# Attention and gated MLP on one core: filling work put ahead of transposes, weight splits one step later, last copies of the first MLP in other buffers

## The chip, the cores and the metric

One core of a Trainium2 chip runs the whole program. The metric is the device time of one execution in microseconds (us); what is compared is the median of several runs. Engines are named as in the profile: PE (TensorE, PEld its weight loads), DVE (VectorE), ACT (ScalarE), POOL (GpSimd), SP (SyncE, which issues the DMAs of this kernel in its own order, SPq in the rows).

## What is computed

```python
def _attn_ref(q, k, v):                      # 8 batches, 8 heads, 576 rows, head size 64
    k_p = k.reshape(B, H, S // 8, 8, D).mean(axis=3)
    v_p = v.reshape(B, H, S // 8, 8, D).mean(axis=3)
    scores = np.matmul(q, k_p.transpose(0, 1, 3, 2)) / np.sqrt(D)
    attn = np.exp(scores - np.max(scores, axis=-1, keepdims=True))
    attn = attn / (np.sum(attn, axis=-1, keepdims=True) + 1e-09)
    return np.matmul(attn, v_p)

def _moe_ref(x, w_gate, w_val, w_out):       # x 4608 x 512, 1536 hidden
    gate = 1.0 / (1.0 + np.exp(-(x @ w_gate)))
    return gate * (x @ w_val) @ w_out

def _moe2_ref(x, w_in, w_out):               # 2048 hidden
    h = x @ w_in
    return np.where(h > 0.0, h, np.exp(np.minimum(h, 0.0)) - 1.0) @ w_out

x = attention(q, k, v) as 4608 rows of 512
out = _moe2_ref(_moe_ref(x, ...), ...)
```

Weights come as 64-bit floats and are narrowed on the chip.

## The kernel before, in words

The 4608 rows are cut into 12 blocks of 384, a block into three tiles of 128. A matmul of full precision is made of three passes of a faster format, with an upper part (a rounded copy, ACT, line 95) and a lower part (source minus upper part, line 96, mostly on POOL). So each weight, each activation `g` and each `x` is "split" before PE can use it.

**Attention of the first two blocks** (lines 617 to 695) comes first and has PE nearly to itself. Per tile `t`: `emit_s` (scores on PE, maximum and subtraction on DVE), `emit_exp` (ACT), `emit_norm` (sum and reciprocal on DVE, product on POOL), `emit_t` (five transposes on PE, split of the transposed probabilities `pt` by ACT and DVE). `between(t)` holds work that fills: pooling K and V by sums of 8 rows (`pool_k`, `pool_v`: five DVE reductions each), `emit_k` (transposes of pooled K, copied to `kbd`), `emit_q`, `place_v` (pooled V spread into masked tiles `vbd` on POOL), and weight conversions. `emit_pv` makes the output `x` of a block.

**Weights of the first MLP** are 36 jobs, three for each of 12 chunks of hidden columns (gate, value, out). A job is loaded as 512 KB of raw words (`fetch`), opened (`open`: ACT takes magnitudes into a tile `nt`), narrowed by four DVE instructions (`narrow_1`, lines 108 and 112; `narrow_2`, lines 118 and 122) and split into `wg` or `wo`. One call of `convert` moves the pipeline by a step: it loads ahead, opens job i+1, does the second half of job i-1 and the first half of job i, and splits job i-1:

```python
            fetch_to(i + 1 + ahead)
            open_to(i + 1 + peek)
            turns = [narrow_2(j.raw, j.t) for j in upto("two", i)] + [narrow_1(j.t) for j in upto("one", i + 1)]
            for _ in range(2):
                for t in turns:
                    next(t, None)
            split_to(i)
```

`nt` has three buffers. Raw words go alternately to the two `raw` buffers and to free `wo` slots, the last five jobs to `raw` alone. The order of the instructions on each engine is that in which the code calls them; engines wait for one another by semaphores.

**First chunk loop** (lines 809 to 830): for each chunk `c`, both gates of block 0 (24 matmuls of 384 columns), three calls of `convert`, the output product of block 0's previous chunk (12), both gates of block 1's previous chunk (24, kept in DRAM as `gd`). That makes 60 matmuls a chunk. Scores of block 2 and block 1's output products (`second_y`, which takes `g` back from DRAM) follow in lines 857 to 877; then come blocks 2 to 11.

**Start of the second MLP** (from line 1021): a step ("slot") is one of seven products of six matmuls (`product`, line 960), then some matmuls from the list `fill`, then what ACT and DVE do behind it (`behind`). In the first seven slots `fill` holds the last 12 output products of the first MLP, from slot 7 on output products of the second (`oacc`, line 1006), which take the accumulators that `flush_y` (lines 537 to 544) empties in slot 6. `flush_y` copies four accumulators to `yo`, a row buffer (4 of them, 3 of which `t_p1`, `t_u2` and `t_u3` hold by then), and stores each to DRAM.

## Time and profile before

| what | us |
|---|---|
| median of 3 runs | 1930.62 (1929.45 to 1930.74) |
| profiled execution | 1932.92, of which span 1931.2 |
| start of the first gate in the profile | 87.14 |
| start of the second MLP in the profile | 1153.48 |

The span runs from the first to the last instruction; what lies around it is 1.7 us. The profiled execution is 2.3 us above the median.

### The profile page before, as it was taken

The page shows a single profiled execution, that of the slowest core. Times are in us where ns is not written, and L with a number is a line of the kernel's source. Part 1 is how long each engine was busy: PE and PEld are TensorE (multiplying, and loading weights), DVE is VectorE, ACT ScalarE, POOL GpSimd, SP SyncE. Part 2 cuts the span into 40 slices and gives each one's busy share as a digit, 9 for nine tenths or more (in the row PEclk, how much of TensorE's full clock was granted, in tenths as well). Part 3 has the DMA queues.
Part 4 walks back from the last instruction along what each step waited for, and adds up shares of the span by engine and source line. Part 5 has one row for each costly group of instructions (what it writes and reads, how often), then busy time and mean ns, then how long its engine had stood idle before and what let it go on. Part 6 is the DMA issues. An engine that isn't in the chain of part 4 may idle for free.

```text
span 1931.2 us, 25883 instructions
## 1 busy us (share of the span) xinstructions
PE 1840.8 (95%) x9996; PEld 1736.9 (90%) x9996; DVE 881.2 (46%) x1455; ACT 793.3 (41%) x1565; POOL 509.0 (26%) x523
## 2 busy tenths in 40 slices
PE   4689789999999999999999997999999999999999
PEld 3589779999999999999999996999989999999997
DVE  6698335454444543455543132443444344443432
ACT  3344224334434343444433233444454444544443
POOL 1454222222113122123222111222222222222222
PEclk7799889999999999999999998999999999999999
DMA  7144223232312322242320424334353343343430
GB/s 185 59 141 150 79 82 90 79 113 71 96 61 80 120 72 77 96 123 91 100 88 28 158 77 188 118 138 160 120 190 123 123 184 115 144 150 144 157 115 33
DMA packets 119227, 218.21 MB, mean 113 GB/s; under 512 B 44352, under 2 KB 76096, under 8 KB 119104
## 3 DMA queue, kind: packets, MB, share of 16 engines
q1 hardware_dynamic: 119104, 216.56, 33.0%
q8 instruction: 78, 1.28, 0.3%
q14 instruction: 45, 0.37, 0.1%
HBM read 172.23 MB, written 44.30 MB: 112 GB/s over the span
## 4 chain that ended last, share of the span: by engine, by line
PE 87%; DVE 4%; DMA 3%; ACT 2%; issue 2%; SPq 1%; POOL 1%; ACTq 0%; DVEq 0%; POOLq 0%
PE gv L507 28%; PE oacc L1006 20%; PE bank L960 18%; PE acc L526 14%; PE atv L487 2%; PE xv L487 2%; PE ats L416 1%; SPq L319 1%; PE att L460 1%; DVE ks L356 1%; PE atq L406 1%; DMA rkv<-in_k_dram 1%; DMA yd<-yo 1%; DMA rkv<-in_v_dram 1%; DVE vs L375 1%
## 5 line engine op out<-in xcount | busy, mean ns | idle before, releaser
L507 PE MATMUL gv<-x,wg 128*128 128x384 f32 x3456 | 643.2, 340 | 14.8 <-ACT sg L515 9.2
L507 PEld LDWEIGHTS gv<-x,wg 128*128 128x128 f32 x3456 | 604.6, 190 | 19.2 <-ACT sg L515 11.1
L1006 PE MATMUL oacc<-w2o,gc 128*128 128x512 f32 x1728 | 453.8, 394 | 1.9 <-DVE yo L541 1.6
L1006 PEld LDWEIGHTS oacc<-w2o,gc 128*128 128x128 f32 x1728 | 320.3, 188 | 50.7 <-DVE yo L541 2.0
L960 PE MATMUL bank<-form,wr 128*128 128x384 f32 x1728 | 355.0, 340 | 9.4 <-ACT p L982 7.9
L960 PEld LDWEIGHTS bank<-form,wr 128*128 128x128 f32 x1728 | 316.1, 189 | 33.1 <-ACT p L982 8.4
L526 PE MATMUL acc<-g,wo 128*128 128x384 f32 x1728 | 331.3, 340 | 8.4 <-ACT g L95 5.7
L96 POOL TENSOR_TENSOR g<-sg,g 128x384 fp32r<-128x384 f32 x132 | 144.3, 1093 | 663.3 <-ACT g L95 663.3
L526 PEld LDWEIGHTS acc<-g,wo 128*128 128x128 f32 x1728 | 304.9, 190 | 12.5 <-ACT g L95 6.4
L519 DVE TENSOR_TENSOR sg<-sg,gv 128x384 f32<-128x384 f32 x132 | 72.5, 549 | 276.1 <-PE gv L507 274.4
L96 POOL TENSOR_TENSOR gc<-ea,gc 128x384 fp32r<-128x384 f32 x96 | 98.0, 1021 | 300.0 <-ACT gc L95 295.9
L96 POOL TENSOR_TENSOR gc<-eb,gc 128x384 fp32r<-128x384 f32 x96 | 98.1, 1022 | 271.4 <-ACT gc L95 250.9
L515 ACT ACTIVATE sg<-gv 128x384 f32<-128x384 f32 x144 | 70.6, 490 | 216.0 <-PE gv L507 213.4
L95 ACT ACTIVATE g<-sg 128x384 fp32r<-128x384 f32 x132 | 69.2, 524 | 158.5 <-DVE sg L519 158.5
L96 DVE TENSOR_TENSOR pt<-att,pt 128x512 fp32r<-128x512 f32 x72 | 34.5, 486 | 119.5 <-ACT pt L95 119.5
L969 ACT ACTIVATE ea<-bank 128x384 f32<-128x384 f32 x48 | 23.6, 492 | 158.4 <-PE bank L960 158.4
L973 DVE SCALAR_TENSOR_TENSOR ea<-ea,bank 128x384 f32<-128x384 f32 x48 | 26.6, 555 | 117.7 <-ACT ea L970 117.7
L969 ACT ACTIVATE eb<-c 128x384 f32<-128x384 f32 x48 | 25.2, 525 | 131.6 <-DVE c L990 131.6
L95 ACT ACTIVATE gc<-eb 128x384 fp32r<-128x384 f32 x96 | 50.4, 525 | 56.6 <-DVE eb L973 33.3
L95 ACT ACTIVATE gc<-ea 128x384 fp32r<-128x384 f32 x96 | 50.5, 526 | 55.4 <-DVE ea L973 55.4
L984 DVE TENSOR_TENSOR u<-p,bank 128x384 f32<-128x384 f32 x48 | 26.6, 554 | 98.9 <-PE bank L960 96.7
L960 PE MATMUL bank<-formx,wr 128*128 128x384 f32 x288 | 58.4, 337 | 0.0
(107 smaller groups left out, 1868.6 us busy)
## 6 DMA issues: line engine op xcount, KB each, us to landing
wr<-wd SPq DMA_DIRECT2D x96, 896.0 KB, 6.2
rw<-in_moe_w_out_dram SPq DMA_DIRECT2D x23, 512.0 KB, 3.8
yd<-yo SPq DMA_DIRECT2D x48, 192.0 KB, 2.1
r<-yd SPq DMA_DIRECT2D x24, 384.0 KB, 8.0
out_dram<-po SPq DMA_DIRECT2D x36, 256.0 KB, 2.0
rw<-in_moe_w_in_dram SPq DMA_DIRECT2D x16, 512.0 KB, 4.5
wd<-rw SPq DMA_DIRECT2D x16, 512.0 KB, 3.3
wod<-rw SPq DMA_DIRECT2D x16, 512.0 KB, 2.7
```

Source lines behind the costliest of these rows:

```text
L95: nc.scalar.activation(out=dst_hi, in_=src, func=AF.Copy)
L96: eng.tensor_tensor(out=dst_lo, in0=src, in1=f32(dst_hi), op=ALU.subtract)
L487: nc.tensor.matmul(d[j][:, o:o + w], lhsT=vb[:m, a_w].rearrange("p e d -> p (e d)"), rhs=p[a_p][:m, j + e, o:o + w], start=(e == 0 and a_w ...
L507: nc.tensor.matmul(d, lhsT=w[:, i, a_w, j], rhs=x[:, a_x, j], start=(j == 0 and a_w == 0 and a_x == 0), stop=(j == KD - 1 and a_w == 1),)
L515: nc.scalar.activation(out=sg, in_=gps, func=AF.Sigmoid)
L519: nc.vector.tensor_tensor(out=sg, in0=sg, in1=vps, op=ALU.mult)
L526: return lambda: nc.tensor.matmul(acc[m], lhsT=wo[c][:, a_w, m * P:(m + 1) * P], rhs=g[:, a_g], start=(c == 0 and a_w == 0 and a_g == 0), ...
L960: nc.tensor.matmul(bank[b ^ flip], lhsT=wp[q][a_w][:, w, j * P:(j + 1) * P], rhs=form_tile(s, a)[j][:, a_x], start=opens and n == 0, stop= ...
L969: nc.scalar.activation(out=e, in_=src, func=AF.Relu, scale=-1.0)
L973: nc.vector.scalar_tensor_tensor(out=e, in0=e, scalar=-1.0, in1=src, op0=ALU.add, op1=ALU.max)
L984: nc.vector.tensor_tensor(out=u2, in0=t_p1, in1=src, op=ALU.add)
L1006: return lambda: nc.tensor.matmul(acc[t + i], lhsT=g[c][:, a_g, i * P:(i + 1) * P], rhs=wo2[2 * q + e][:, a_w], start=opens and p == 0, st ...
```

## The change

Six edits.

1. The first three weight jobs are loaded earlier: job 0 ahead of all keys, job 1 ahead of the queries, job 2 ahead of the second block's keys. Seven instead of five conversions are done before the first chunk loop.
2. In the attention of the first two blocks, `emit_exp` and `between(t)` stand ahead of `emit_t(t - 1)`; what `between` holds is dealt out anew.
3. `convert` begins with the split of job i-2 instead of ending with that of job i-1. Every fourth `nt` is a row buffer (`ntr`).
4. Even jobs at the end also load to free `wo` slots.
5. In `second_y`, the split of `g` stands ahead of the tile's `emit_exp`.
6. `flush_y` of the last block is due in slot 3; its last three copies go to `nt` buffers (`yn`); all 12 fill matmuls are issued in slot 3, none in the other slots before 7.

```diff
+    turn = [0]
+    def first_t():
+        turn[0] += 1
+        return row_tile("ntr", DM).bitcast(I32) if turn[0] % 4 == 0 else plain_t()
@@ fetch_to
-            if i % 2 or i > 3 * C1 - 6:
+            if i % 2:
                 job.raw = raw_tile("rw")
@@ convert
+            split_to(i - 1)
             fetch_to(i + 1 + ahead)
...
-            split_to(i)
@@ flush_y
-            t = row_tile("yo", NB)
+            if n == NBLK - 1 and m:
+                t = act.tile([P, DM], F32, name="yn", tag="nt", bufs=3)[:, :NB]
+            else:
+                t = row_tile("yo", NB)
@@ loads
+        fetch_to(1)
         load_all("k", 0, k0, l0[:, 0])
+        fetch_to(2)
         for i in range(TPB):
             load_q(i, q0[:, i])
+        fetch_to(3)
         load_all("k", 1, k1, l1[:, 0])
-        fetch_to(1)
...
+        convert(1, 0, 0)
         for c in range(NCH):
             pool_k(0, c)
         emit_k(0)
+        open_to(2)
         for i in range(TPB):
             emit_q(i, qt[0][:, i])
+        convert(1, 0, 0)
@@ between
             if t == 0:
+                convert(1, 1, 0)
+            elif t == 1:
                 for c in range(NCH):
                     pool_k(1, c)
-            elif t == 1:
+            elif t == 2:
                 emit_k(1)
-                for c in range(3):
-                    pool_v(0, c)
-            elif t == 2:
-                convert(1, 2)
-                for c in range(3, NCH):
+                for c in range(NCH):
                     pool_v(0, c)
...
-                convert(1, 2)
-                for j in range(HP):
-                    place_v(0, j)
+                place_v(0, 2)
+                place_v(0, 3)
+                convert(1, 1)
@@ tiles
             scores = emit_s(t, ph[t])
+            emit_exp(scores)
+            between(t)
             if t > 0:
                 emit_t(t - 1, True)
-            emit_exp(scores)
-            between(t)
             emit_norm(t, scores)
-            if t == TPB:
+            if t == TPB - 1:
+                place_v(0, 0)
+                place_v(0, 1)
+            elif t == TPB:
                 emit_pv(0)
@@ second_y
                     load_g(done + 2)
+                if then:
+                    then()
+                    then = None
                 if pend:
                     last_y()
...
-            emit_exp(scores)
-            second_y(1)
+            second_y(1, lambda: emit_exp(scores))
@@ second MLP
-        due = {6: [lambda: flush_y(pn, pacc)]}
+        due = {3: [lambda: flush_y(pn, pacc)]}
...
-                    filler(-(-len(fill) // (7 - k)))
+                    filler(len(fill) if slot == 3 else -(-len(fill) // (7 - k)) if slot > 6 else 0)
```

On DVE, at tile 1 of the attention, before: maximum and subtraction of the scores, then at once the split of tile 0's transposed probabilities (`pt`).

```order
L424 TENSOR_REDUCE mx<-ats 128x8
L427 TENSOR_TENSOR p_211<-ats,mx 128x576
L96 TENSOR_TENSOR pt<-att_251,pt 128x4x128
L96 TENSOR_TENSOR pt<-att_252,pt 64x128
L370 COPY kbd_126<-atk 64x4x72
L375 TENSOR_REDUCE vs<-v_133 128x64 x3
L438 TENSOR_REDUCE sm<-p_211 128x8
```

The same place in the changed kernel:

```order
L431 TENSOR_REDUCE mx<-ats 128x8
L434 TENSOR_TENSOR p_225<-ats,mx 128x576
L363 TENSOR_REDUCE ks<-k_131 128x64 x4
L363 TENSOR_REDUCE ks<-l_136 64x64
L96 TENSOR_TENSOR pt<-att_275,pt 128x4x128
L96 TENSOR_TENSOR pt<-att_276,pt 64x128
L445 TENSOR_REDUCE sm<-p_225 128x8
```

The five reductions of block 1's keys now stand between the subtraction and the split of `pt`; the copy `kbd` and the sums of V have gone to tile 2.

On ACT, in the first chunk loop, from the split of block 0's second `g` on, before:

```order
L95 ACTIVATE g<-sg 128x384
L190 ACTIVATE nt<-rw 128x512
L95 ACTIVATE wg_767<-nt 128x512
L515 ACTIVATE sg<-gv 128x384 x2
L190 ACTIVATE nt<-rwo 128x512
L95 ACTIVATE wg_767<-nt 128x512
```

And in the changed kernel:

```order
L95 ACTIVATE g<-sg 128x384
L95 ACTIVATE wg_763<-nt 128x512
L197 ACTIVATE nt<-rw 128x512
L522 ACTIVATE sg<-gv 128x384 x2
L95 ACTIVATE wo_845<-ntr 128x512
L197 ACTIVATE nt<-rwo 128x512
```

The upper part (`wg`, `wo`) stood behind the opening of the next job and right ahead of the sigmoids (`sg`); now it is that of a job one step older, ahead of the opening.

On PE, slots 3 to 5 of the second MLP, before (line 960 is `product`, line 526 the first MLP's output products):

```order
L960 MATMUL bank_10033<-form_9860,wr_9549 128x384 x2
L960 MATMUL bank_10033<-form_9860,wr_9550 128x384
L526 MATMUL acc<-g,wo_1696 128x384 x2
L960 MATMUL bank_10032<-form_9910,wr_9549 128x384 x2
L960 MATMUL bank_10032<-form_9910,wr_9550 128x384
L960 MATMUL bank_10032<-form_9910,wr_9549 128x384 x2
L960 MATMUL bank_10032<-form_9910,wr_9550 128x384
L526 MATMUL acc<-g,wo_1696 128x384 x2
```

And in the changed kernel:

```order
L978 MATMUL bank_10033<-form_9860,wr_9549 128x384 x2
L978 MATMUL bank_10033<-form_9860,wr_9550 128x384
L533 MATMUL acc<-g,wo_1624 128x384 x12
L978 MATMUL bank_10032<-form_9910,wr_9549 128x384 x2
L978 MATMUL bank_10032<-form_9910,wr_9550 128x384
L978 MATMUL bank_10032<-form_9910,wr_9549 128x384 x2
L978 MATMUL bank_10032<-form_9910,wr_9550 128x384
```

All twelve matmuls of the first MLP's last output now stand behind slot 3's product, and none behind slot 4's.

## Rows read from the trace of the kernel before

**Rows 1.** The page: busy time of each engine over the span.

```profile
PE 1840.8 (95%) x9996; PEld 1736.9 (90%) x9996; DVE 881.2 (46%) x1455; ACT 793.3 (41%) x1565; POOL 509.0 (26%) x523
```

**Rows 2.** Windows: length, busy us (instructions) of each engine, PEclk, DMA share, GB/s.

```profile
core 0: us, PE busy (x) PEld busy (x) DVE busy (x) ACT busy (x) POOL busy (x), PEclk, DMA share, GB/s
0.00:87.14 87.14, 40.37 (x193) 33.53 (x193) 53.57 (x84) 29.43 (x71) 27.70 (x47) 0.72 0.47 127
87.14:117.73 30.59, 25.07 (x121) 23.82 (x121) 26.85 (x38) 13.61 (x25) 13.27 (x9) 0.89 0.37 120
117.73:180.96 63.23, 63.07 (x361) 62.75 (x361) 58.20 (x84) 28.12 (x55) 35.57 (x24) 1.00 0.49 158
...
189.35:213.64 24.29, 16.60 (x74) 15.95 (x74) 10.64 (x16) 6.39 (x12) 8.63 (x7) 0.79 0.35 98
233.44:281.61 48.17, 38.42 (x196) 35.22 (x196) 16.47 (x26) 15.91 (x36) 15.09 (x15) 0.89 0.37 111
1153.48:1187.16 33.68, 22.72 (x101) 19.90 (x101) 9.03 (x16) 10.82 (x20) 5.78 (x6) 0.80 0.28 103
1187.16:1202.70 15.54, 15.54 (x79) 14.02 (x78) 4.82 (x9) 6.52 (x13) 3.67 (x4) 1.00 0.88 360
```

**Rows 3.** Timeline, attention: start, us, engine, line, operation, [idle before <-releaser].

```profile
6.71 3.79 DVE L356 TENSOR_REDUCE ks<-k 128x64 f32<-128x512 f32 x4 [3.57 <-DMA k<-in_k_dram]
...
49.57 3.81 PE L487 MATMUL atv<-pt,vbd 128*128 128x384 f32 x12 [5.49 <-POOL vbd L386]
...
87.14 10.29 PE L507 MATMUL gv<-x,wg 128*128 128x384 f32 x48 [0.48 <-DVE x L96]
```

**Rows 4.** Windows: DMA rate while the first keys land.

```profile
3.00:6.00 3.00, 0.00 (x0) 0.00 (x0) 0.14 (x1) 0.00 (x0) 0.11 (x1) 1.00 1.00 354
```

**Rows 5.** Timeline: DVE narrowing, without and with POOL at work.

```profile
45.33 0.67 DVE L118 SCALAR_TENSOR_TENSOR nt<-rwo,nt 128x512 int32<-128x512 int32 x1
45.93 0.41 DVE L108 TENSOR_SCALAR nt<-nt 128x512 f32<-128x512 f32 x1
...
114.97 1.60 POOL L96 TENSOR_TENSOR wg<-nt,wg 128x512 fp32r<-128x512 f32 x1 [4.24 <-ACT wg L95]
115.34 1.52 DVE L112 TENSOR_SCALAR nt<-nt 128x512 int32<-128x512 int32 x1
```

**Rows 6.** Waits of DVE up to 87 us: total, times, longest.

```profile
DVE pt L96 <- ACT pt L95: 6.8, 5, 1.7
```

**Rows 7.** Timeline: the first chunks' stalls of PE.

```profile
105.31 2.37 PE L507 MATMUL gv<-x,wg 128*128 128x384 f32 x12 [2.48 <-DVE sg L519]
...
108.74 0.63 ACT L95 ACTIVATE wg<-nt 128x512 fp32r<-128x512 f32 x1 [1.02 <-DVE nt L122]
...
109.80 6.01 PE L507 MATMUL gv<-x,wg 128*128 128x384 f32 x24 [2.12 <-ACT sg L515]
```

**Rows 8.** Timeline: the last weight jobs.

```profile
196.37 3.79 PE L507 MATMUL gv<-x,wg 128*128 128x384 f32 x12 [2.66 <-DVE sg L519]
...
203.59 0.66 ACT L190 ACTIVATE nt<-rw 128x512 f32<-128x512 f32 x1 [3.93 <-DMA rw<-in_moe_w_out_dram]
...
205.19 6.52 PE L507 MATMUL gv<-x,wg 128*128 128x384 f32 x24 [5.03 <-ACT sg L515]
```

**Rows 9.** Timeline: block 1's output products, first tile.

```profile
240.39 0.62 PE L526 MATMUL acc<-g,wo 128*128 128x384 f32 x1 [2.77 <-ACT g L95]
...
242.53 1.00 POOL L96 TENSOR_TENSOR g<-rg,g 128x384 fp32r<-128x384 f32 x1
```

**Rows 10.** Timeline: start of the second MLP.

```profile
1160.76 1.33 PE L960 MATMUL bank<-form,wr 128*128 128x384 f32 x6 [1.41 <-DVE ea L973]
...
1168.67 10.12 SPq L544 DMA_DIRECT2D yd<-yo  x4
...
1175.32 0.49 ACT L543 ACTIVATE yo<-acc 128x384 f32<-128x384 f32 x1 [6.68 <-DMA yd<-yo]
...
1179.90 2.29 PE L960 MATMUL bank<-form,wr 128*128 128x384 f32 x6 [7.93 <-ACT p L982]
```

More of the change, by code (lines that the diff above doesn't have):

```diff
@@ L166, in dst_o @@
             return wo[c][:, 0], wo[c][:, 1]
-        jobs.append(Job(cols(w_gate, c), plain_t, halves(pair(0))))
-        jobs.append(Job(cols(w_val, c), plain_t, halves(pair(1))))
-        jobs.append(Job(rows(w_out, c), plain_t, halves(dst_o)))
+        jobs.append(Job(cols(w_gate, c), first_t, halves(pair(0))))
+        jobs.append(Job(cols(w_val, c), first_t, halves(pair(1))))
+        jobs.append(Job(rows(w_out, c), first_t, halves(dst_o)))
     def upto(step, n):
@@ L627, in fused_kernel @@
             load_q(TPB + i, q1[:, i])
-        fetch_to(2)
+        fetch_to(4)
         load_all("v", 1, v1, l1[:, 1])
-        fetch_to(3)
+        fetch_to(5)
         make_identity(nc, ident)
@@ L842, in fused_kernel, with second_y @@
         done = 0
-        def second_y(n):
+        def second_y(n, then=None):
             nonlocal done, pend
```

## The prediction, made before the changed kernel was timed

> **What bounds the kernel now.** I read the busy shares first: PE is busy 1840.8 of 1931.2 us [rows 1], so the 90 us in which it isn't, and stretches at a lower clock, are all that an edit of order can win. Then the windows [rows 2]. Two of them are the measure for the others: 117.73 to 180.96 (PE 63.07 of 63.23, clock 1.00, 361 matmuls, so 0.175 us for one of 384 columns) and 1187.16 to 1202.70, seven slots of the second MLP in 15.54 us, 2.22 us each. The five others are where the change works. In the attention (87 us) PE works 40 at a clock of 0.72, and DVE 53.6: nobody is full, the time is a chain of waits. In the first chunks 121 matmuls, 21.2 us at the measure, take 30.6. From 189.35 to 213.64 the code has 72, or 12.6 us, and takes 24.3. Block 1's output products (233.44 to 281.61) lose 9.8 us of idle PE, at a clock of 0.89. The start of the second MLP, 33.7 us for eleven slots, runs at 0.80. Everything else is the measure itself and isn't touched.
>
> **The change, part by part.**
>
> *Attention.* The end of this stretch is the first gate at 87.14. What delays it now: the first keys would land later, since the 0.52 MB of job 0 go ahead of them at 354 GB/s [rows 4], 1.5 us behind the 6.71 of [rows 3]. Two more conversions (job 5 and 6) have to fit: four DVE instructions each, two as L118 (0.67) and two as L108 (0.41) [rows 5], 2.16 us, so 4.3. For it: DVE waited 6.8 us, in five waits of up to 1.7, for ACT's copy of the transposed tile [rows 6], and now has work ahead of that. I walked the new DVE order through the tiles with the durations of the trace: first scores 1.4 us later; new waits of 2.0 us at the second `kbd` (its transposes need the score accumulator, read just before) and 2.6 us at tile 1's `pt` (ACT first has five V copies and three of queries); block 0's output product, at 49.57 now [rows 3], 3.0 later; block 1's scores 4 later. The tail gets it back: the last tile's probabilities no longer wait for GpSimd behind a split and two `vbd`, and block 1's later `vbd` start sooner, as the split in front of them is that of an older job. The sum comes out within 0.5 us of 87.14. I take 0, with -3 (all of the 6.8 less loads and conversions) and +4 (nothing given back) as ends.
>
> *First chunks.* Two stalls stand there [rows 7]. PE waits 2.48 for the product on DVE, which stands behind five conversions; there are as many in the new order, so this stays. It waits 2.12 for a sigmoid, which ACT runs behind the split at 108.74, which waited 1.02 for DVE's L122. That split is now of a job that DVE finished a call earlier, and the fourth `nt` takes away ACT's wait for POOL to free one. I take -2 (about that stall), between 0 and -5: with it could go the lower clock behind it, 24 matmuls in 6.01 us instead of 4.2, and part of the first stall.
>
> *The last jobs.* All five went to two `raw` buffers, so each load waited for the job two ahead, and ACT for the load: 3.93 us at 203.59, with PE waiting 2.66 and 5.03 for what stands behind [rows 8]. With `wo` slots for jobs 32 and 34 a buffer is free two calls ahead, as in the stretch where PE never waits. The window loses 24.3 - 12.6 = 11.7; I take -11, at worst -7 (one of the two stalls stays with its lower clock).
>
> *Block 1's output products.* The first stall, 2.77, is `g` behind the exponential on ACT [rows 9]. Now `g` goes first, but the next `g` still stands behind the tile's sum on ACT and its product on POOL, whose lower part ended at 243.5 [rows 9]; PE would do 12 matmuls and wait for that. It gains the 11 that ran behind 241.5 at a lower clock. The later two tiles end on the same POOL chain. I take -1.5, from -3 to +0.5.
>
> *Start of the second MLP.* `flush_y` has one free row buffer, so copy 2 waits for store 1 and so on: ACT 6.68 us in one wait, the four stores spread over 10.12 us on SP, PE 7.93 for the copy behind them [rows 10]. With three `nt` buffers, which nothing else uses there, no copy waits. By the new order the first slots are: three products (3.2 us), the fourth (1.05), 12 fills (2.1). PE is there at 1153.5 + 6.4 = 1159.9. The wait of 1.41 that ends at 1160.76 [rows 10] is for slot 2's exponential; slot 2 now ends 0.7 sooner, without the four fills ahead of it, so what PE waits for is there at 1160.0. Slots 4 to 6 have no fill: products of 1.05 us follow each other, and slot 7 waits for DVE, some 1.2 us, as the subtraction of slot 5 stands behind the second ELU. Slot 7 then starts 0.7 us sooner than at 1164.91 and slots 7 to 10 take 4 x 2.22, so slot 11 begins at 1173.4 instead of 1187.16. That is -13.8. I take -13.5, from -11.5 to -14.2 (no wait at slot 7). The twelve fills in one place hide that exponential; if it came later, the 1.41 and the 0.7 would be back, 2.1 us.
>
> The moved `place_v` cost nothing: POOL does eight while PE waits for the last tile of block 0.
>
> **Sum:** 0 - 2 - 11 - 1.5 - 13.5 = -28. The profiled 1932.9 becomes 1904.9; the median stands 2.3 below the profiled execution, so 1902.6 us, 1.45% less.
>
> **One row that speaks against it.** L112 took 1.52 us instead of 0.41 while POOL's split ran [rows 5]. In the full stretch, 6.04 chunks of 10.47 us, DVE is busy 58.20 us, 9.64 a chunk, of which 3 x 2.16 + 1.1 = 7.6 would be its work alone [rows 2]; so POOL already costs it 2, and 0.8 is left before DVE, not PE, sets the pace. Splits that start at other moments could hit more. The Trainium skill (SBUF — State Buffer, "Reading the diagram" of its ports) says that VectorE and GpSimd share one pair of ports by an exclusive lock: whoever starts first holds it for the whole instruction. By that rule taken to its end it would be the second rival; the trace agrees only in part, 2 of the 5.9 us that POOL works in a chunk.
>
> **Rivals.**
> 1. *The last loads stay late*: the `wo` slot for job 34 comes free only with job 30's narrowing, so if a load lands in more than a call and a half, ACT waits again. For it: ACT waited for loads there at all. Against: `raw` buffers had the same distance all through the full stretch. Only 4 of 11 are won: 1909.6. Chance 0.12.
> 2. *DVE becomes the bound of the chunk loop*, slower than before: each of POOL's four subtractions blocks a DVE instruction wholly, 7.6 + 35.57/6.04 = 13.5 us a chunk, 3.0 above PE's; nine chunks give +27, and the two added conversions in the attention, four instructions at +1.1, +4.4: 1902.6 + 31.4 = 1934. It decides from 13.1 us a chunk up, where 9 x 2.6 + 4.4 uses up the 28. Against: the upper copy still follows DVE's narrowing of the same job, so POOL starts near the same DVE instructions as now. Chance 0.04; in between (half a microsecond a chunk, 1907) lies within the range.
> 3. *The attention pays*: the keys of block 0 wait for three weight loads (1.57 MB, 4.4 us) instead of one, and the tail gives nothing back: +4 + 2.9, 1909.5. For it: PE at a clock of 0.72 and DMA queues that share engines. Against: only job 0 is issued ahead of the first keys, and they are what the first DVE sums wait for. Chance 0.14.
> 4. *The stores aren't what holds slot 9*: the copies are free but `r` and `wr` loads behind them on SP come late for the next slots: half of 13.5, 1909. Against: they are needed seven slots later. Chance 0.07.
>
> **Numbers.** My forecast has 0.60, and 0.03 is left for no change to be measured, a sum of small failures. Its own range is 1897 to 1908 (attention -3/+4, the others within their bounds, not all at one end). Rivals 1, 3 and 4 lie about 1909, so 1896 to 1912 holds more than 8 in 10. A measurement here tells about 0.2%, 4 us. Faster by more: 0.93 (forecast, rivals 1, 3 and 4); within: 0.03; slower: 0.04 (rival 2).
>
> **What would show it.** In the changed profile: no DVE wait of 1 us for ACT at the first `pt`, but one ahead of the second `kbd`; the first gate between 84 and 91; PE without gaps over 1 us from the third chunk on, the loop's end about 13 us sooner against the first gate; four copies of the last `flush_y` within 2 us, and slots 8 to 11 at 2.2 us. Wrong if the first gate is later than 92, if a chunk takes more than 10.6 us, or if PE still waits for a load's job near the end of the loop.

## The result, and the profile after

The changed kernel takes 1906.63 us, the median of four runs (1902.59, 1907.35, 1905.92, 1908.79), against 1930.24 of four of before: a ratio of 0.9876 (95% interval 0.9858 to 0.9893). The forecast was 1902.6, with a range from 1896 to 1912. The profiled execution is the quickest of the four: 1902.59 us, span 1900.9, against 1932.9 and 1931.2. So the profiles lie 30.3 us apart and the medians 23.6; why these differ is a question of its own below.

The windows of the same stages, as in [rows 2] (the start of the second MLP is now 1136.60 to 1156.80):

```profile
core 0: us, PE busy (x) PEld busy (x) DVE busy (x) ACT busy (x) POOL busy (x), PEclk, DMA share, GB/s
0.00:87.36 87.36, 40.77 (x192) 34.11 (x192) 62.10 (x92) 30.67 (x74) 31.10 (x48) 0.73 0.48 134
87.36:115.30 27.94, 23.11 (x121) 22.47 (x122) 26.12 (x35) 13.37 (x24) 14.07 (x10) 0.94 0.41 134
115.30:188.00 72.70, 72.70 (x413) 71.47 (x413) 72.42 (x97) 32.81 (x62) 40.33 (x27) 1.00 0.50 161
187.38:200.37 12.99, 12.94 (x74) 12.43 (x73) 6.56 (x9) 3.29 (x7) 7.14 (x6) 1.00 0.19 47
220.17:265.36 45.19, 35.57 (x197) 32.41 (x197) 16.47 (x26) 15.93 (x36) 15.08 (x15) 0.96 0.39 118
1136.60:1156.80 20.20, 19.45 (x102) 17.54 (x102) 8.94 (x16) 10.73 (x20) 5.58 (x6) 1.00 0.60 221
1156.80:1172.34 15.54, 15.54 (x79) 14.02 (x78) 4.83 (x9) 6.54 (x13) 3.92 (x5) 1.00 0.76 296
```

The attention has the length it had (87.36 for 87.14) with 8.5 us more of DVE in it; the first chunks are 2.7 us shorter, the former stretch of the last jobs 11.3 (12.99 for 24.29), block 1's output products 3.0 (45.19 for 48.17), the start of the second MLP 13.5 (20.20 for 33.68). One stage got longer, and only the third window shows it: where DVE was busy 58.20 of 63.23 us, it is now busy 72.42 of 72.70. In the chunk loop DVE is full.

The timeline of the attention and the first chunks (start, us, engine, line, operation, [idle before <-releaser]) answers to [rows 3, 7]:

```profile
8.27 3.78 DVE L363 TENSOR_REDUCE ks<-k 128x64 f32<-128x512 f32 x4 [1.89 <-DMA k<-in_k_dram]
...
36.51 0.46 DVE L377 COPY kbd<-atk 64x288 f32<-64x288 f32 x1 [2.06 <-ACT kbd L376]
...
43.99 0.88 DVE L96 TENSOR_TENSOR pt<-att,pt 128x512 fp32r<-128x512 f32 x2 [2.24 <-ACT pt L95]
...
50.42 0.66 PE L494 MATMUL atv<-pt,vbd 128*128 128x384 f32 x1 [1.74 <-POOL vbd L393]
52.17 3.89 PE L494 MATMUL atv<-pt,vbd 128*128 128x384 f32 x11 [1.10 <-DVE pt L96]
...
78.76 2.82 PE L494 MATMUL atv<-pt,vbd 128*128 128x192 f32 x12
...
87.36 6.54 PE L514 MATMUL gv<-x,wg 128*128 128x384 f32 x36 [0.33 <-DVE x L96]
94.99 2.38 PE L514 MATMUL gv<-x,wg 128*128 128x384 f32 x12 [1.09 <-DVE sg L526]
...
105.30 8.08 PE L514 MATMUL gv<-x,wg 128*128 128x384 f32 x36 [3.73 <-DVE sg L526]
```

The first keys are summed 1.56 us later (8.27), DVE waits 2.06 at the second `kbd` and 2.24 at tile 1's `pt`, block 0's output product starts 0.85 later with one matmul (50.42) and 2.6 later with the others (52.17): 1.5, 2.0, 2.6 and 3.0 were forecast. The wait for a sigmoid, 2.12 in [rows 7], is gone; the wait for DVE's product, 2.48 there, is now 1.09 in the first chunk and 3.73 in the second.

The start of the second MLP, which answers to [rows 10]:

```profile
1140.93 2.25 PE L533 MATMUL acc<-g,wo 128*128 128x384 f32 x12
...
1143.52 1.02 DVE L551 COPY yn<-acc 128x384 f32<-128x384 f32 x2
1143.60 0.47 ACT L553 ACTIVATE yo<-acc 128x384 f32<-128x384 f32 x1
...
1143.97 0.48 ACT L553 ACTIVATE yn<-acc 128x384 f32<-128x384 f32 x1
...
1144.51 1.37 SPq L554 DMA_DIRECT2D yd<-yn  x3
...
1147.34 1.32 PE L978 MATMUL bank<-form,wr 128*128 128x384 f32 x6 [0.72 <-DVE u L1011]
```

The twelve fills stand in slot 3, the four copies run between 1143.52 and 1144.5 on two engines, and SP issues their stores from 1144.10 to 1145.9, not over 10 us. Nothing waits for a store; the one wait of PE is the 0.72 at slot 7, forecast as 1.2.

Added up between the two profiled executions: attention +0.2, first chunks -2.7, nine chunks from the third on 95.5 for 106.4 us (-10.8), from there to block 2's product of values 54.5 for 57.5 (-3.0), the blocks up to the second MLP -0.6, its first eleven slots -13.5: -30.3.

### The profile page after: what moved, and what is told of

Same layout as the page of the kernel before. It is cut to its first block, busy times and chain, and to the rows that moved or that the text cites. A ratio compares the mean times of both kernels' runs of the same rounds, so it can differ in the third digit from the quotient of the medians.

```text
span 1900.9 us, 25876 instructions
## 1 busy us (share of the span) xinstructions
PE 1830.2 (96%) x9996; PEld 1726.8 (91%) x9996; DVE 891.7 (47%) x1455; ACT 792.7 (42%) x1565; POOL 511.5 (27%) x523
## 4 chain that ended last, share of the span: by engine, by line
PE 89%; DVE 5%; ACT 2%; DMA 2%; issue 1%; POOL 1%; SPq 0%; ACTq 0%; DVEq 0%; POOLq 0%
PE gv L514 29%; PE oacc L1024 21%; PE bank L978 19%; PE acc L533 14%; PE atv L494 2%; PE xv L494 2%; PE ats L423 2%; DVE ks L363 1%; PE atq L413 1%; PE att L467 1%; DMA rkv<-in_v_dram 1%; DVE vs L382 1%; DMA rkv<-in_k_dram 1%; DMA k<-in_k_dram 0%; DVE nt L118 0%
## 5 line engine op out<-in xcount | busy, mean ns | idle before, releaser
L533 PE MATMUL acc<-g,wo 128*128 128x384 f32 x1728 | 327.4, 337 | 7.3 <-POOL g L96 4.2
L526 DVE TENSOR_TENSOR sg<-sg,gv 128x384 f32<-128x384 f32 x132 | 72.5, 550 | 277.7 <-PE gv L514 276.0
L987 ACT ACTIVATE ea<-bank 128x384 f32<-128x384 f32 x48 | 23.6, 492 | 156.4 <-PE bank L978 156.4
L95 ACT ACTIVATE gc<-eb 128x384 fp32r<-128x384 f32 x96 | 50.4, 525 | 53.3 <-DVE eb L991 31.4
```

Of the source, the lines that this page charges most:

```text
L95: nc.scalar.activation(out=dst_hi, in_=src, func=AF.Copy)
L526: nc.vector.tensor_tensor(out=sg, in0=sg, in1=vps, op=ALU.mult)
L533: return lambda: nc.tensor.matmul(acc[m], lhsT=wo[c][:, a_w, m * P:(m + 1) * P], rhs=g[:, a_g], start=(c == 0 and a_w == 0 and a_g == 0), ...
L987: nc.scalar.activation(out=e, in_=src, func=AF.Relu, scale=-1.0)
```

## The experiments

Times are medians, each ratio is to runs of the kernel before on the same chip. This table is from PE's timeline in the one profiled execution of each: start of block 1's product of values, first gate, third chunk, tenth run of gates of the loop (the twelfth chunk's), block 2's product of values, and that execution's time.

| kernel | values 1 | first gate | third chunk | tenth run | values 2 | us |
|---|---|---|---|---|---|---|
| before | 77.38 | 87.14 | 117.73 | 224.10 | 281.61 | 1932.9 |
| changed | 78.76 | 87.36 | 115.30 | 210.84 | 265.36 | 1902.6 |
| e1_again | 79.72 | 88.47 | 116.42 | 211.91 | 266.42 | 1903.0 |
| e2_old_flush | 78.99 | 90.21 | 119.97 | 215.46 | 272.25 | 1921.3 |
| e3_old_raw | 79.50 | 88.25 | 116.20 | 220.24 | 276.27 | 1913.0 |
| e4_old_split | 78.00 | 88.00 | 118.92 | 213.47 | 270.44 | 1907.8 |
| e5_old_exp | 79.71 | 88.46 | 116.40 | 212.02 | 269.43 | 1907.5 |
| e6_old_attention | 74.01 | 85.22 | 115.74 | 211.60 | 266.13 | 1903.4 |
| e7_low_on_dve | 81.98 | 90.61 | 121.75 | 225.53 | 281.55 | 1918.2 |
| e8_g_on_dve | 78.98 | 90.20 | 120.00 | 215.58 | 268.85 | 1906.1 |
| e9_extra_matmuls | 73.93 | 83.59 | 113.21 | 208.67 | 265.77 | 1901.0 |
| e10_low_dve_late | 81.18 | 89.79 | 121.00 | 215.20 | 271.04 | 1908.4 |
| e11_buffers_alone | 79.56 | 90.78 | 120.56 | 216.03 | 271.84 | 1910.4 |
| e12_combined | 73.39 | 82.62 | 110.55 | 204.75 | 258.02 | 1894.8 |

**The changed kernel once more.** No edit.

> The changed kernel itself, unedited, for its spread and a second profile. Its four runs lay between 1902.6 and 1908.8 us, wider than the 1929.4 to 1930.7 of before. Theory: the spread comes from the first chunk loop, where VectorE is now busy 72.4 of 72.7 us, so each collision with GpSimd costs time; another execution has its first gate at 87 +- 0.5 and its second MLP as in the first profile, but the nine chunks from the first run of 48 gate matmuls to the tenth take another time than 95.5 us, by about what its total differs. Rival: the attention varies (first gate off by 2 us or more), with the chunks at 95.5 +- 0.5. Time for both: 1906.6 +- 3.

1904.95 (1902.98 to 1911.07, four runs), ratio 0.9871 (0.9855 to 0.9888). The spread is there again, and the profile again caught the quickest execution, so by itself this run showed no cause for it. But by the table the nine chunks take 95.5 to 95.6 us in all six profiles of kernels that are the same up to the loop's end (the changed kernel, e1, e2, e5, e8, e11), while their third chunk starts anywhere from 115.30 to 120.56. What varies there lies ahead of the nine chunks and not in them, as the theory had it.

**The last flush as before.**

```diff
-            if n == NBLK - 1 and m:
-                t = act.tile([P, DM], F32, name="yn", tag="nt", bufs=3)[:, :NB]
-            else:
-                t = row_tile("yo", NB)
+            t = row_tile("yo", NB)
...
-        due = {3: [lambda: flush_y(pn, pacc)]}
+        due = {6: [lambda: flush_y(pn, pacc)]}
...
-                    filler(len(fill) if slot == 3 else -(-len(fill) // (7 - k)) if slot > 6 else 0)
+                    filler(-(-len(fill) // (7 - k)))
```

> Edit 6 undone (the last copies in row buffers, due in slot 6, fills spread over seven slots), the rest as changed. Theory: the start of the second MLP gives the whole 13.5 us that the two profiles show there, so 1920 against 1906.6, and the stall of 7.9 us ahead of slot 9 is back. Rival: part of it comes from elsewhere (other loads on the queue ahead of slot 9): +7 or less.

1920.46, ratio 0.9941 (0.9928 to 0.9953), 13.8 and 15.5 us above the changed kernel's two medians. The wait of [rows 10] is back in PE's timeline:

```profile
1169.38 2.29 PE L975 MATMUL bank<-form,wr 128*128 128x384 f32 x6 [7.96 <-ACT p L997]
```

**Buffers alone.** As above, but with the `yn` tiles kept.

> Of the last part of the change only the other buffers: block 5's four output copies lie in tiles of their own, but stay at slot 6, and the output products that fill the first slots are spread as before. By the steps of the prediction the buffers carry nearly all of the 13.5 us (a stall of 7.9 and of 6.7 us, the fourth is small), and the earlier slot is worth what the copies wait for at slot 6: 1907 to 1910, with the stall ahead of the product of slot 9 gone or under 2 us. Rival (the stores still arrive too late from slot 6, and the slot is what decides): a stall of 4 us or more remains and the time is 1914 to 1920, as with the whole part undone.

1906.19, ratio 0.9872 (0.9855 to 0.9888), that of the changed kernel. Slot 8 starts 13.8 us after the first product (1143.79 to 1157.60), in the changed kernel 13.1 (1136.77 to 1149.90). (The expectation's "block 5" is the last block.) So the buffers are the whole of the gain but for 0.7 us; slot 3 in place of slot 6 and the gathered fills are worth that much.

**The last jobs' buffers as before.**

```diff
-            if i % 2:
+            if i % 2 or i > 3 * C1 - 6:
                 job.raw = raw_tile("rw")
```

> Edit 4 undone (the last five jobs again in the two raw buffers), the rest as changed. Theory: the two stalls of PE near the loop's end come back, +11 us, 1917.5; ACT waits some 4 us for loads again. Rival: with seven conversions ahead of the loop and the splits a step later, the last loads are early enough anyway: +3 or less, 1909.

1915.03, ratio 0.9919 (0.9905 to 0.9932), 8 to 10 us above the changed kernel. PE's timeline has one long wait near the loop's end:

```profile
191.08 6.26 PE L514 MATMUL gv<-x,wg 128*128 128x384 f32 x24 [6.87 <-ACT sg L522]
```

PE waits 6.87 us for a sigmoid, and the 24 gates behind it take 6.26 us at a granted clock of 0.68: the nine chunks take 104.0 us, for 95.5.

**The upper parts at the old step.** The fourth tile on `row` goes too.

```diff
-            split_to(i - 1)
...
+            split_to(i)
...
-        return row_tile("ntr", DM).bitcast(I32) if turn[0] % 4 == 0 else plain_t()
+        return plain_t()
```

> Edit 3 undone (split of the job just narrowed at the end of a conversion, three narrowing tiles), the rest as changed. Theory: the stall of 2 us behind ACT's sigmoid in the first chunks is back (+2.7), but GpSimd's splits meet VectorE as before, so that nine chunks take 94.3 instead of 95.5 us and the spread shrinks: +1 to +2, 1908. Rival: the later split is what keeps the loop going at all with the two extra conversions: +5 or more. Second rival: it does nothing, within 0.5.

1906.99, ratio 0.9869 (0.9854 to 0.9884): no difference in the time, made of two that about cancel. The third chunk starts 30.9 us behind the first gate, with a wait of 1.03 for a sigmoid again (27.9 in the changed kernel, 29.8 in the profiles whose first gates ran, as here, partly at the lower clock); the nine chunks take 94.55 us, for 95.5. DVE's groups by line in the middle of the loop (names, shapes xcount | busy us, mean ns | idle before), first of the changed kernel, then of this one:

```profile
L112 DVE TENSOR_SCALAR nt<-nt 128x512 int32<-128x512 int32 x14 | 11.3, 806 | 0.0
L122 DVE SCALAR_TENSOR_TENSOR nt<-rwo,nt 128x512 int32<-128x512 int32 x10 | 10.4, 1036 | 0.0
L108 DVE TENSOR_SCALAR nt<-nt 128x512 f32<-128x512 f32 x13 | 9.8, 751 | 0.0
L118 DVE SCALAR_TENSOR_TENSOR nt<-rwo,nt 128x512 int32<-128x512 int32 x9 | 9.1, 1009 | 0.1
```

```profile
L112 DVE TENSOR_SCALAR nt<-nt 128x512 int32<-128x512 int32 x19 | 20.8, 1097 | 0.0
L122 DVE SCALAR_TENSOR_TENSOR nt<-rwo,nt 128x512 int32<-128x512 int32 x10 | 10.1, 1013 | 0.0
...
L108 DVE TENSOR_SCALAR nt<-nt 128x512 f32<-128x512 f32 x19 | 8.0, 421 | 0.1
...
L118 DVE SCALAR_TENSOR_TENSOR nt<-rwo,nt 128x512 int32<-128x512 int32 x10 | 7.2, 716 | 0.1
```

With the split behind the narrowing, POOL's subtraction meets one DVE operation (L112, 1.10 us for 0.41) and partly L122; with the split ahead of the next narrowing it is spread over all four. All tiles together, a tile costs DVE 3.5 us instead of 3.25, and three tiles a chunk fill it: while weights are converted, DVE's product L526 returns every 10.7 us (137.62 to 191.00, five chunks), where PE needs 10.47.

**The exponential ahead of g again.**

```diff
-            second_y(1, lambda: emit_exp(scores))
+            emit_exp(scores)
+            second_y(1)
```

> Block 1's output products with the softmax's exponential ahead of the split of g again, all other parts of the change kept. The step of the prediction (it gives 1.5 us, bounds -3 to +0.5; the two profiles show 3.0 there) expects the product of values and probabilities of block 2 to start 1.5 to 3 us later after the loop's tenth run of gates than the 54.5 us of the changed kernel, and a time of 1906 to 1909 where the changed kernel has 1905 to 1906.6. The rival, that POOL's norm product takes the place of the wait anyway (its releases now stand ahead of output products with 1.56 and 1.53 us), expects no difference over 1 us in that stretch.

1907.04, ratio 0.9882 (0.9868 to 0.9895). From the tenth run of gates to block 2's values it takes 57.4 us, for 54.5; in the time these 2.9 are within the spread. And one profile of each doesn't size the edit: nine of the profiles in the table have the changed code in this stretch, and it takes 54.5 us in three of them (the changed kernel, e1, e6), 55.8 to 56.0 in three (e3, e10, e11) and 56.8 to 57.1 in three (e2, e4, e9). PE's waits for the parts of `g` are the same in sum, 7.4 us here and 7.3 in the changed kernel. What differs is the clock behind them, in PE's timeline of this kernel, then of the changed one, then of e4, which has the changed order too:

```profile
228.29 0.44 PE L533 MATMUL acc<-g,wo 128*128 128x384 f32 x1 [2.77 <-ACT g L95]
229.43 5.86 PE L533 MATMUL acc<-g,wo 128*128 128x384 f32 x23 [0.69 <-POOL g L96]
...
254.53 8.91 PE L533 MATMUL acc<-g,wo 128*128 128x384 f32 x35 [0.39 <-POOL g L96]
```

```profile
230.16 2.19 PE L533 MATMUL acc<-g,wo 128*128 128x384 f32 x11 [1.56 <-POOL g L96]
...
251.46 7.91 PE L533 MATMUL acc<-g,wo 128*128 128x384 f32 x35 [0.64 <-POOL g L96]
```

```profile
255.52 8.93 PE L533 MATMUL acc<-g,wo 128*128 128x384 f32 x35 [0.39 <-POOL g L96]
```

Here 23 output products took 5.86 us behind the waits of 2.77 and 0.69 (granted clock 0.71), and 35 took 8.91, for 7.91 in the changed kernel. But e4 has 8.93 for the same 35: that difference comes with the execution, not with the edit.

**g's lower part on DVE in block 1's output products.**

```diff
-                    split(g[:, 0], g[:, 1], g_raw.pop(done))
+                    split(g[:, 0], g[:, 1], g_raw.pop(done), nc.vector)
```

> In block 1's output products alone the lower part of g is subtracted on DVE (9 of 25 us busy there) and no longer on POOL, behind whose norm product it stood. Theory: the two stalls of 1.56 and 1.53 us that POOL's g releases and the one of 0.64 go or fall under 0.5, the stretch from the loop's tenth run of gates to block 2's product of values falls from 54.5 to 51 to 53 us, and the time by 2 to 3.5 us. Rival: the stalls are set by the exponential on ACT or by the loads of g, they keep their length under another releaser, and the time is the same within 1 us.

1904.53, ratio 0.9869 (0.9855 to 0.9882). The waits for POOL, 1.56 and 1.53, became waits for DVE of 0.79 and 0.85, but the two ahead of the first (0.45 and 0.98) became one of 1.93: the stretch takes 53.3 us (e12, with the same edit, too), under all nine profiles of the changed code there (54.5 to 57.1). Against the quickest of them these 1.2 us are less than expected, and they are not to be told in the time.

**The attention and its loads in the old order.** Edits 1 and 2 are undone: the order of the loads, the two more conversions, what `between` holds and the order in a tile. The later split and everything behind the attention stay.

> The loads' order and the whole order of the first two blocks' attention as before (five conversions instead of seven, transposes ahead of the next tile's fill), the parts behind it kept. The prediction's steps expect 0 from the attention itself (first gate at 86 to 88 us of the profile) and the first chunks to give back what the two more conversions gained: the first run of 48 gates starts 2 to 5 us later relative to the first gate than the 27.9 us of the changed kernel, so 1907 to 1911. The rival, that the attention's new order pays by itself, expects a first gate over 2 us later; the other rival, that late upper parts alone made the gain of the first chunks, expects the run of gates at the same place and the time the same within 1 us.

1898.87 (1895.48 to 1903.37, five runs), ratio 0.9838 (0.9822 to 0.9855): none of the three expectations. It is the quickest yet, some 6 to 8 us under the changed kernel. PE's timeline:

```profile
45.40 4.02 PE L494 MATMUL atv<-pt,vbd 128*128 128x384 f32 x12 [0.52 <-POOL vbd L393]
...
74.01 2.85 PE L494 MATMUL atv<-pt,vbd 128*128 128x192 f32 x12
...
85.22 8.70 PE L514 MATMUL gv<-x,wg 128*128 128x384 f32 x36
```

Block 0's output product waits 0.52 us for POOL's `vbd`, where before it waited 5.49 [rows 3], and starts at 45.40 for 49.57. Its attention is that of before; what differs ahead of it is the later split (with its fourth tile). With the old split and the new order (e4) the same product waits 2.80 for `vbd` and starts at 51.32. So the later split alone takes 3.4 us off the start of block 1's values (77.38 to 74.01), and the new order (loads, attention and the two more conversions; they weren't told apart) puts about 5 on (74.01 to between 78.76 and 79.72). But the two edits don't add. With the old split the new order costs only 0.6 (77.38 to 78.00, e4), and with the new order the later split gains nothing (78.00 to between 78.76 and 79.72). POOL's timeline shows why, before, then here, in e4 and in the changed kernel:

```profile
47.68 1.26 POOL L96 TENSOR_TENSOR wg<-nt,wg 128x512 fp32r<-128x512 f32 x1 [4.99 <-ACT wg L95]
48.90 4.61 POOL L386 TENSOR_TENSOR vbd<-vhl,mask 128x256 fp32r<-128x256 f32 x8
```

```profile
43.45 5.69 POOL L393 TENSOR_TENSOR vbd<-vhl,mask 128x256 fp32r<-128x256 f32 x8
```

```profile
47.09 5.92 POOL L393 TENSOR_TENSOR vbd<-vhl,mask 128x256 fp32r<-128x256 f32 x8
```

```profile
47.26 5.87 POOL L393 TENSOR_TENSOR vbd<-vhl,mask 128x256 fp32r<-128x256 f32 x8
```

Before, block 0's `vbd` stood behind the split of a weight. The later split moves that one out of the way, and so does the new order, which places `vbd` ahead of the conversion: in each of the last three kernels the `vbd` follow POOL's product of the probabilities of block 0's last tile at once. What one edit has won the other can't win again, and the new order delays that product itself (42.35 here, 45.98 in e4, 46.15 in the changed kernel). At the same clock level this kernel is still 4 us ahead at the tenth run (211.60; e2, e8 and e11 have 215.46 to 216.03), and e12, whose first gates ran at a granted clock of 1.00, starts them at 82.62, for 87.36 to 88.47 in the changed kernel, e1, e3 and e5. The rest of the 6 to 8 isn't placed: the profile caught the slowest of the five executions.

**The lower parts of the weights on DVE.**

```diff
-            split(hi, lo, t.bitcast(F32))
+            split(hi, lo, t.bitcast(F32), nc.vector)
```

> The lower part of each narrowed weight tile of the first MLP is subtracted on DVE and no longer on POOL, all else as in the changed kernel. Theory (DVE bounds nine chunks at 95.5 us because its narrowing operations run beside POOL's subtractions: 0.81, 0.75, 1.0 and 1.0 us a tile, alone 0.41 and 0.67): the four operations fall to about 2.2 us a tile, a subtraction of 0.7 comes on top, so some 2.9 instead of 3.5 us a tile, 2.7 tiles a chunk: DVE has 9 us in a chunk and the nine chunks take 94.2 us (10.47 each); the wait of 3.73 for DVE's product in the second chunk falls by half or more; in all -1.5 to -4 us. Rival (the narrowing operations are slow by themselves there, for instance by the loads' landing beside them): they keep 3.5 us a tile, the subtraction comes on top, a chunk takes 12 us, the loop 108, and the time rises by 10 to 15 us.

1919.61, ratio 0.9948 (0.9936 to 0.9961). The theory was wrong, and the rival had the time but not its cause: the nine chunks take 103.8 us, 11.5 each, though the narrowing operations fell to their price without POOL. DVE's groups, as above:

```profile
L96 DVE TENSOR_TENSOR wg<-nt,wg 128x512 fp32r<-128x512 f32 x9 | 8.2, 913 | 7.0 <-ACT wg L95 7.0
L118 DVE SCALAR_TENSOR_TENSOR nt<-rwo,nt 128x512 int32<-128x512 int32 x10 | 6.8, 681 | 0.0
```

The subtraction stands ahead of the narrowing and waits for ACT's upper part, 7.0 us here and 8.6 in two more groups, and the narrowing queues behind it. It isn't work that fills DVE (72.91 of the 96 us from 116 on) but order.

**The same, behind the narrowing of the step.**

```diff
-            split(hi, lo, t.bitcast(F32))
+            s = t.bitcast(F32)
+            nc.scalar.activation(out=hi, in_=s, func=AF.Copy)
+            lowers.append(lambda: nc.vector.tensor_tensor(out=lo, in0=s, in1=f32(hi), op=ALU.subtract))
...
                 for t in turns:
                     next(t, None)
+            lower()
```

> As the changed kernel, with the lower part of the narrowed weights subtracted on DVE, but behind the four narrowing operations of the same step and no longer ahead of them. Theory (in the run with the subtraction ahead of them DVE lost 17 us of 74 waiting for ACT's upper parts, while the narrowing operations fell to 2.2 us a tile): with ACT's copy out of the way the wait goes, a tile costs DVE 2.2 + 0.7 to 0.9 us, a chunk 8 to 9.2 of 10.47, the nine chunks take 94.2 to 94.8 us where the changed kernel has 95.5; the time is 1902 to 1906. Rival (DVE's part of a chunk is too long in any order, or a step's later end holds the gates): chunks of over 11 us, and a time over 1910.

1908.34, ratio 0.9884 (0.9871 to 0.9898). The loop is as the theory had it: 94.2 us, every chunk 10.47, a tile 2.2 + 0.7 on DVE. What that won was lost again ahead of the loop. The third chunk starts 31.2 us behind the first gate, for 27.9, since PE waits 5.74 for POOL's lower part of the first `g`. POOL's, DVE's and PE's timelines:

```profile
98.64 7.65 POOL L96 TENSOR_TENSOR g<-sg,g 128x384 fp32r<-128x384 f32 x1 [10.54 <-ACT g L95]
...
98.52 0.42 DVE L108 TENSOR_SCALAR nt<-nt 128x512 f32<-128x512 f32 x1
...
106.34 3.89 PE L543 MATMUL acc<-g,wo 128*128 128x384 f32 x11 [5.74 <-POOL g L96]
```

One subtraction took POOL 7.65 us (the next one 1.18), for as long as DVE's operations followed each other without a gap and at their full speed: fifteen from 97.92 on. In the chunks behind, where DVE's runs are shorter, POOL's subtraction of `g` takes 2.72 us.

**More matmuls in the waits** (on the kernel with the old attention; their result isn't read).

```diff
+        def warm(n):
+            d = ps.tile([P, NB], F32, name="xv", tag="gv", bufs=2)
+            for i in range(n):
+                nc.tensor.matmul(d, lhsT=x_t[0][:, 0, 0, 0:P], rhs=x_t[0][:, 0, i % KD], start=True, stop=True)
...
+            if t == 2 * TPB - 1:
+                warm(28)
...
+        warm(34)
         emit_t(2 * TPB - 1, True)
```

> The kernel with the old order of the attention and all later parts of the change, and with 62 matmuls of 128x384 whose result nobody reads, put into TensorE's two waits ahead of block 1's product of values and probabilities (28 into the wait of 6.74 us, 34 into the one of 7.80). Theory (which executions are slow is set by the level of TensorE's clock in that product and the first gates: 36 gates in 6.5 us or in 8.4 to 8.7, four runs of 12 matmuls in 8.4 or in 11.7): with the engine busy in the waits the upper level is granted there each time, the product starts at 74 us as without them, its four runs take 7 to 9 us, the first gates start at 81 to 83 us and 36 of them take 6.5; the time is 1893 to 1898 with a spread of 3 us or less, where the kernel without them had 1895.5 to 1903.4. Rival (the level is not set by what TensorE did just before): the same runs as without them, or the matmuls delay the transposes behind them: 1899 or more, and the spread stays at 8 us.

1901.11 (1896.15 to 1901.44), ratio 0.9837 (0.9824 to 0.9851): no faster than without. PE's timeline:

```profile
73.93 1.56 PE L494 MATMUL atv<-pt,vbd 128*128 128x192 f32 x12
...
79.24 1.59 PE L494 MATMUL atv<-pt,vbd 128*128 128x192 f32 x6 [1.39 <-POOL vbd L393]
80.64 3.00 PE L494 MATMUL xv<-pt,vbd 128*128 128x192 f32 x12
83.59 9.16 PE L514 MATMUL gv<-x,wg 128*128 128x384 f32 x36
```

The first half of the product ran at the upper level (granted clock 1.00; 12 matmuls in 1.56 us, for 2.85), came to the point where POOL's `vbd` wasn't ready, and after 1.39 us of waiting the rest and the gates ran at the lower (0.50 from 79.2 to 88.0; 36 in 9.16).

**Together**: the old attention, g of block 1 on DVE, and the lower parts of weights and g on DVE, late, from the tenth tile and the third chunk on.

> The old order of the loads and of the attention with all later parts of the change, and with three lower parts moved from POOL to DVE: of the narrowed weights from the tenth tile on and of block 0's g from its third chunk on (each behind the narrowing operations of its step), and of g in block 1's output products. Theory (what the single runs showed adds up): against the old order alone (1898.9) the nine chunks take 94.2 instead of 95.9 us, the output products 1.2 us less, so 1894 to 1897; the first chunks stay as they were, since DVE's additional work begins behind them. Rival: DVE, which runs in order, stands before ACT's copies again or has too much with g, chunks of over 10.7 us and a time at or above 1899.

1897.79 (1894.76 to 1900.44, five runs), ratio 0.9834 (0.9819 to 0.9848). The nine chunks take 94.2 us, and the window has room on DVE and nothing on POOL:

```profile
115.00:188.00 73.00, 73.00 (x420) 73.00 (x419) 63.06 (x126) 33.86 (x63) 0.00 (x0) 1.00 0.52 167
```

It is the lowest median, some 8 us under the changed kernel, but from the old attention alone (0.9838) the measurement doesn't tell it.

## Why the prediction was right, and where it wasn't

**Start of the second MLP, -13.5.** Right, 13.5, and by the mechanism named: e2 gives it back, e11 shows that it is the buffers. Rival 4 fell. The sum itself has a slip: 1164.91 less 0.7, and four slots of 2.22, is 1173.1 and not 1173.4, so -14.1. Slot 7 did come 0.7 sooner, but slots 7 to 10 took 9.46 us in place of 8.88.

**The last jobs, -11.** Right; e3 gives 8 to 10 back in the time, 8.5 in the loop. Rival 1 fell. The stretch itself won 11.3; the nine chunks together 10.8.

**Block 1's output products, -1.5.** Not refuted. The one profile gives 3.0 and e5 2.9, but the changed code took 54.5 to 57.1 us there in nine profiles, 55.8 on the mean, and the old order 57.5 and 57.4 in its two: 0.3 to 3.0, and 1.7 against the mean. That POOL's norm product takes the place of the exponential was right (the sum of the waits is 7.3 for 7.4), and so was that what is won is clock. I counted only the 11 products behind the first wait; which other products run lower differs between executions of the same code (the 35 behind the last wait take 7.91 us in the changed kernel and 8.93 in e4).

**First chunks, -2.** The amount was right (-2.65 in the profile), the parts were not. The sigmoid's wait went with the later split, as reckoned (it is back with 1.03 in e4). But part of the -2.65 is clock: the first 36 gates ran in 6.54 us in the profiled execution, and in others in 8.4. From first gate to third chunk it takes 27.9 us where these 36 gates have a granted clock of 1.00 (the changed kernel, e1, e3, e5), and 29.8 where they have 0.76 (e2, e8, e11). The two conversions done ahead are worth nothing that shows: with the old attention, which has two fewer, it takes 27.9 (e12, 36 gates in 6.85).

**Attention, 0.** As a sum it came out, +0.2, and the waits are those I had listed: `kbd` 2.06, `pt` 2.24, the keys 1.56; block 1's scores came 3.4 later (59.01 for 55.66), where I had 4, and the tail gave most of it back. In part that is luck: the same code has its first gate at 87.4 to 88.5 in four profiles and at 90.2 to 90.8 in three, by the clock. And the sum hid what a part is worth. I had credited POOL's earlier `vbd` to the moved `place_v` and to the older split alike, but either of them has it without the other: with the later split and the old order block 1's values start at 74.01, with the new order and the old split at 78.00, with both at 78.76 to 79.72. Beside the later split the new order wins nothing and costs about 5 (e6 beside e2 at the same clock level: 74.01 and 78.99, 85.22 and 90.21 for the first gate). What I lacked was the question which edit each compensation belonged to. Which of the loads, the two conversions and the order in a tile brings the cost isn't shown. The third rival, "the attention pays", had the sign and a chance of 0.14, but looked for the loss in the first gate against before, where it doesn't show. The times agree: the three runs with the old order (e6, e9, e12) have ratios from 0.9834 to 0.9838, six with the new one (the changed kernel, e1, e4, e5, e8, e11) 0.9869 to 0.9882.

**DVE in the loop.** My sum put this at nothing, and the row that spoke against the change was right. Splits at other moments hit more of DVE's instructions (e4 beside the changed kernel), DVE became full, nine chunks take 1.3 us more than PE needs. That is rival 2 with 0.15 us a chunk in place of 3. The chunk is 10.6 us on the mean and 10.7 while weights are converted, so one of my own signs of being wrong, a chunk of more than 10.6, came by a hair. With the lower parts of the weights off POOL it goes (e10, e12: 94.2): DVE's four operations fall from 3.5 to 2.2 us a tile, which shows that the meeting of the two engines is the cause.

**Why the medians lie closer than the profiles.** Between executions the clock at block 1's values and the first gates differs. The changed kernel and e2 are the same up to this place, and e2's timeline has:

```profile
78.99 2.85 PE L494 MATMUL atv<-pt,vbd 128*128 128x192 f32 x12
...
90.21 8.36 PE L514 MATMUL gv<-x,wg 128*128 128x384 f32 x36
```

Against 78.76 and 87.36 above: 36 gates in 8.36 us and not 6.54, the third chunk at 119.97 and not 115.30. In three profiles (e2, e8, e11) the product ran at a granted clock of 0.50 and the 36 gates at 0.76, and the third chunk starts at 119.97 to 120.56; in four (the changed kernel, e1, e3, e5) they had 0.83 to 0.85 and 1.00, and it starts at 115.30 to 116.42. 4.7 us are about what separates 1902.6 from 1907.4; for the executions without a profile that is argued, not shown. Block 1's output products are a second such place, 54.5 to 57.1 us in the same code, and the changed kernel's profile has the quick end of both. So the step of the forecast that was mis-sized is its last one: it went from the profiled execution to the median with an offset of 2.3 that the old kernel had, and the changed one has 4.0 the other way. What decides the level in one execution stays open: e9 kept TensorE at work in the waits, and the level still fell. The old kernel's executions differ as well: 1929.45 to 1930.74 in the four, but 1929.16 to 1933.11 in nine beside e1 and 1928.03 to 1934.73 in nine beside e5.

## What to carry to other kernels

Where a step's zero is a sum of gains and losses, ask of each which edit brings it, and undo the edits one by one even if the total is as forecast: here one part of a change that won 24 us cost 6 to 8 beside the others. Two edits that go at the same wait don't add, so undo them singly and together before saying what each is worth. An engine that runs in order is filled by its waits as much as by its work: the same subtraction cost 1.1 us a chunk ahead of the narrowing and nothing behind it. And before a median is forecast from a profile, look at whether the stretches at a lower clock are the same in every execution.

## What the runs showed of the hardware

DVE can keep POOL waiting over many instructions, not one: 7.65 us for a subtraction of 1.18 beside a gapless run of fifteen DVE instructions of 0.42 to 0.69 us (e10), and from the other side POOL lengthens DVE's instructions, 1.10 us for 0.42 (L112, e4 and e10). The Trainium skill (SBUF — State Buffer, "Reading the diagram") has one shared pair of ports, held for a whole instruction by whichever of the two starts first. The rows agree that the loser is blocked, but in e10 for far longer than one instruction; how POOL came to get no turn between DVE's instructions no run here shows.

TensorE's clock is not a property of the program alone: the same 36 matmuls took 6.52 to 6.54 us (granted clock 1.00) or 8.36 to 8.39 (0.76) in profiles of kernels that are the same up to there. The Trainium skill (TensorE: Matmul & The Clock Gate, Part 1) puts the level down to how busy the engine has been. In e9, 62 matmuls in the waits brought the upper level to the first half of a product and not to the gates behind it; no run here shows what decides between the two in executions of the same code.
